# Moving a weight load, two sets of transposes and a pair of copies in a fused attention and MLP kernel

## The chip, the core and the metric

The kernel runs on one core of one Trainium2 chip. The metric is the device time of one execution in microseconds (us); lower is better. Three runs of the kernel before took 360.17, 360.77 and 361.07 us, so its median is 360.77 us.

## The reference, cut to what matters

The input x has 2048 rows of D = 576 channels in bf16. A transformer block is computed: an attention part over a short dilated window with 32 heads of 18 channels, and an MLP of 4608 hidden channels.

```python
def _A_ref(x, wqkv, wo):                       # W, dil = 8, 2
    q, k, v = split(x @ wqkv)                  # 32 heads of 18 channels
    idx = pos[:, None] - arange(W)[None, :] * dil     # 8 keys, two rows apart
    logits = einsum(q, k[idx]) * scale         # masked where idx < 0
    return einsum(softmax(logits), v[idx]) @ wo

def _B_ref(x, w1, b1, w2, b2):
    return gelu(layernorm(x) @ w1 + b1) @ w2 + b2

h = A_x + _A_ref(layernorm(A_x), A_wqkv, A_wo)
out = h + _B_ref(layernorm(h), B_w1, B_b1, B_w2, B_b2)
```

## The kernel before

**Tiles.** The 2048 rows are cut into 16 tiles j of 128 rows, where tile j holds the rows j, 16 + j, 32 + j and so on. The key that lies 2w rows back is then in tile j - 2w, on the same partition or on the one before it. The keys and values of the even tiles and of the odd tiles stand in two rings; a "halo" load, through DRAM, replaces a tile's rows by the same rows one partition down when the tiles behind it need them.

**Stages.** First come 24 "visits" on TensorE (numbered 0 to 23 in the code, each of two duos, a duo being one 128-row tile times one of Wq, Wk, Wv), until about 66 us. Into them the attention of the first two tiles, A[0] and A[1], and their LN2 are worked in. Then eight groups of two tiles pass through the MLP: MLP1 (line 228, tile `pm`) in four visits, then MLP2 (lines 605 and 693, tile `po`). Within the MLP of group k, VectorE (DVE) does the attention of group k + 1, whose tiles are named c and d in the code. Their output projection ("wo", tile `pw`) is put in the middle of group k's MLP.

**A visit.** TensorE works with its array cut into an upper and a lower half of 64 rows, which compute two banks of PSUM at once. `phase` (lines 221 to 235) issues the matmuls of one duo: phase 0 with ten matmuls, then, after phase 0 of the other duo, phase 1 with eight matmuls and the halves exchanged. Phase 1 may start only after phase 0 of the same duo has ended; that is signalled by an empty instruction in GpSimd's (POOL's) queue (`marker`, line 238). A duo ends with its eviction by ScalarE (ACT, line 322 for Q, K and V). A hook runs after all phases 0; a `between` list runs after phase 1 and the eviction of the duo that it names (a plain list: of the first duo). The duos' banks go round a ring of three, C, A, B; bank D is left to transposes and wo.

**Transposes by TensorE.** The attention output of A[0] and A[1] is transposed by `tr_o` (line 433): four blocks of 128 channels, and a last block of the channels 512 to 575, which must stand twice, once for each half of the array. For this, `o_tail` (line 197) first lets ScalarE copy these 64 channels twice into a tile `tail` of 128 columns. Ten small matmuls then fill the tile `o_pt`, and ScalarE evicts it to `oT`. The normalized h of the two tiles, `hn`, is transposed by `tr_h` (line 556), which uses `transpose_tail` (line 185): here no copy is made. Eight matmuls (line 188) transpose the four blocks, two more the channels 448 to 575, whose upper half is right, and two further ones (line 192, on a quarter of the array) overwrite the lower half with the channels 512 to 575. ScalarE evicts the tile `h_pt` to `hnT` (line 559), which the first MLP1 matmul reads for both tiles. Later tiles are stored to a DRAM scratch `td` by two DMAs (lines 210, 211: 144 KB and 16 KB) and read back by a transposing DMA (lines 216, 447, 516).

**Queues around the change.** All five engines run in the order in which the code issues instructions (`manual_schedule`). Around the change:

- Visit 16: phases 0, `tr_o(A[0])` as hook, phases 1. ScalarE has `o_tail(A[0])`, the eviction of `o_pt`, then those of the duos.
- Visits 19 and 21, `between`: LN2's root of A[0] and A[1] on GpSimd (line 161), then on ScalarE the mean (line 541) and the normalized row (line 174).
- Visit 22: phases 0, `tr_h(A[0])` as hook, phases 1; `att_exp(A[2])` on ScalarE between its two evictions. Visit 23: phases 0, `tr_h(A[1])` as hook, phases 1. MLP1 of group 0 follows.
- Group 0, second visit of MLP1: SyncE's (SP's) queue gets the store and transposed read of the attention output of c, a halo load of d, the last piece of W2 (`load_w2(6)`, 576 KB, four of the 36 row blocks of W2), then the store and transposed read of the attention output of d. A transposed read waits in the queue until the store has landed.
- Group 0, MLP2 of its first tile: before row block 0 wo of c is finished, and before row block 19 stands the visit of wo of d, which reads what the second transposed read brought. The last piece of W2 is first read at row block 32 of this tile.

Of the kernel before, what the change touches and what calls it, by code (L numbers as in the profile page):

```python
# [11 lines left out]
BF16 = mybir.dt.bfloat16  # L12
# [5 lines left out]
def kernel(  # L18
# [12 lines left out]
    nc = tc.nc  # L31
    P = 128
    _, S, D = A_x.shape
# [5 lines left out]
    KT = 5  # L39
    KF = 4  # L40
# [5 lines left out]
    HP = P // 2  # L46
# [130 lines left out]
    def transpose_in(pair, src, tail=None):  # L177
        for kt in range(KT):
            c = min(kt * P, D - P)
            block = src[:, c:c + P] if kt < KF or tail is None else tail  # L180
            for r in range(2):
                nc.tensor.matmul(pair[:, r, kt * HP:(kt + 1) * HP], lhsT=block[half_rows(r)],
                                 rhs=ident[half_rows(r), half_rows(r)], start=True, stop=True, skip_group_check=True)

    def transpose_tail(pair, src):
        for kt in range(KF):
            for r in range(2):
                nc.tensor.matmul(pair[:, r, kt * HP:(kt + 1) * HP], lhsT=src[half_rows(r), kt * P:(kt + 1) * P],
                                 rhs=ident[half_rows(r), half_rows(r)], start=True, stop=True, skip_group_check=True)
        for c, rows in ((D - P, slice(None)), (KF * P, half_rows(0))):  # L190
            for r in range(2):
                nc.tensor.matmul(pair[rows, r, KF * HP:KT * HP], lhsT=src[half_rows(r), c:c + P if rows.start is None else D],
                                 rhs=ident[half_rows(r), half_rows(r)], start=True, stop=True, skip_group_check=True)

    o_tails = {}

    def o_tail(j):
        o_tails[j] = qp.tile([P, 2, HP], BF16, tag="tail", name="tail", bufs=2)
        nc.scalar.copy(out=o_tails[j][:], in_=q_all[:, j, KF * P:D].unsqueeze(1).to_broadcast([P, 2, HP]))

    def turned(dst, pair, k0=0, k1=KT):
        return dict(out=dst[:, k0:k1, :].rearrange("p k (r t) -> p r k t", r=2),
# [15 lines left out]
    def half_rows(r):  # L218
        return slice(r * HP, (r + 1) * HP)
# [335 lines left out]

    def tr_h(j, tag):
        pair = psum_pair(tag, "h_pt")
        transpose_tail(pair, hn.pop(j)[:])
        nc.scalar.copy(**turned(hnT_slot(j), pair))

    def gelu_table():
# [143 lines left out]
    def c_(fn, *a):  # L705
        return lambda: fn(*a)
# [100 lines left out]
    with tc.manual_schedule(engines={ENG.PE, ENG.Activation, ENG.DVE, ENG.SP, ENG.Pool}):  # L807
# [93 lines left out]
        A = ATT_ORDER  # L901
# [38 lines left out]
        for v, fns in ((2, [(load_w1, 0)]), (3, [(load_w1, 1)]), (4, [(load_w1, 2)]), (6, [(load_wo, [0])]), (8, [(load_wo, [1, 2])]),  # L940
# [25 lines left out]
        between = {  # L966
            10: [c_(att_exp, A[0])],
            13: [c_(att_exp, A[1])],
            18: [c_(o_tail, A[1])],
            19: {0: [c_(ln2_rstd, A[0])], 1: [c_(ln2_norm, A[0])]},  # L970
            21: {0: [c_(ln2_rstd, A[1])], 1: [c_(ln2_norm, A[1])]},
            22: [c_(att_exp, A[2])],
        }
        wo_with = {17: A[0], 20: A[1]}
        hooks = {
            0: {1: lambda: call([c_(tr_x, EVEN[1], "C"), c_(ln1_even, 2)])},
            **{n: {m: c_(tr_x, EVEN[2 * n + m - 1], "D" if m == 1 else None) for m in (1, 2)} for n in (1, 2, 3)},
            12: c_(tr_b1, "D"),
            16: c_(tr_o, A[0], "D"),
            19: c_(tr_o, A[1], "D"),  # L980
            22: c_(tr_h, A[0], "D"),
            23: c_(tr_h, A[1], "D"),
        }
        seq = [(j, t) for t in (1, 2) for j in EVEN[:2]] + [(j, 1) for j in EVEN[2:]] \
# [53 lines left out]
        for k, g in enumerate(GROUPS):  # L1038
# [11 lines left out]
            if k == 0:  # L1050
                m1[0] += [c_(halos, 1), c_(load_w2, 5), c_(att_qk_a, d), c_(att_qk_rest, d, 1), c_(halo, d, 1)]
                mid[0] = {1: [c_(exps, d)]}
                m1[1] = [c_(pv_t, c), c_(att_den, d), c_(att_pv_a, d), c_(halo, d, 2), c_(load_w2, 6), c_(att_pv_b, d),
                         c_(dma_tr_o, d), c_(add_b2, g[0]), c_(add_b2, g[1]), c_(att_qk_a, e), c_(halo, e, 1)]
                late_wo = wo_duo(c, "B")
                ia[0] = [c_(ln2_h, c), c_(ln2_act, c), c_(put_b2, c), c_(halos, 2), c_(ln2_send, c), c_(att_qk_b, e, 0)]
                ia[19] = [lambda d=d: wo_visit((d, "A"), fill=True), c_(ln2_h, d), c_(ln2_act, d), c_(put_b2, d), c_(ln2_in, c),
                          c_(att_max, [e]), c_(att_qk_a, f), c_(ln2_send, d), c_(ln2_in, d), c_(halo, f, 1), c_(att_qk_rest, f, 1),
                          c_(exps, e, f)]
                ib[0] = [c_(finish_out, g[0]), c_(out_sum, g[0]), c_(att_den, e, f), c_(pv_sum, e), c_(send_o, e)]  # L1060
                ib[8] = [c_(read_o, e)]
            elif k == 1:
                m1[0] += [c_(att_pv_sum, d), c_(send_o, d), c_(halo, d, 2)]
                m1[1] += [c_(att_qk_a, e), c_(halo, e, 1), c_(read_o, d), c_(att_qk_b, e, 0), c_(halos, 7)]
                m1[3] += [c_(out_store, GROUPS[0][0]), c_(att_qk_a, f), c_(halo, f, 1), c_(att_qk_add, f, ((0, 0, 9), (0, 0, 4)))]
                ia[0] = [c_(wo_visit, (c, "B"), (d, "C")), c_(ln2_pair, c, d), c_(att_qk_b, f, 1, 2), c_(att_max, (e, f)),
                         c_(exps, e, f), c_(w2_sums, 0, 8, (0, 1)), c_(w2_sums, 8, 12, (0, 1)), c_(att_den, e, f)]
                ia[2] = [c_(pv_sum, e), c_(dma_tr_o, e), c_(reload_x, GROUPS[4])]
                ib[0] = [c_(finish_out, g[0]), c_(out_sum, g[0])]
# [94 lines left out]
```

## Time and profile before

| what | value |
|---|---|
| median of three runs | 360.77 us |
| the profiled execution | 361.01 us |
| its span, first to last instruction | 359.2 us |
| TensorE busy | 353.4 us (98% of the span) |
| VectorE busy | 295.8 us (82%) |
| ScalarE busy | 235.8 us (66%) |
| GpSimd busy | 47.3 us (13%) |
| granted TensorE clock | 1.000 |

The span is 1.8 us shorter than the execution that it comes from, and that execution is 0.24 us over the median. The chain of waits, the list of work followed back from the last instruction, shows VectorE from about 10 to 84 us and TensorE for nearly all that follows. In the timelines a row has its start in us, its length in us, the engine, the line, the operation with its output and inputs, how many instructions are merged into the row, and in brackets how long the engine stood idle before it and what ended that. PE is TensorE's matmuls and PEld its weight loads, SPq and POOLq are the queues in which SyncE and GpSimd issue.

### The profile page before, as it was taken

The page shows a single profiled execution, that of the slowest core. Times are in us where ns is not written, and L with a number is a line of the kernel's source. Part 1 is how long each engine was busy: PE and PEld are TensorE (multiplying, and loading weights), DVE is VectorE, ACT ScalarE, POOL GpSimd, SP SyncE. Part 2 cuts the span into 40 slices and gives each one's busy share as a digit, 9 for nine tenths or more (in the row PEclk, how much of TensorE's full clock was granted, in tenths as well). Part 3 has the DMA queues.
Part 4 walks back from the last instruction along what each step waited for, and adds up shares of the span by engine and source line. Part 5 has one row for each costly group of instructions (what it writes and reads, how often), then busy time and mean ns, then how long its engine had stood idle before and what let it go on. Part 6 is the DMA issues. An engine that isn't in the chain of part 4 may idle for free.

```text
span 359.2 us, 11579 instructions
## 1 busy us (share of the span) xinstructions
PE 353.4 (98%) x4953; PEld 289.5 (81%) x4953; DVE 295.8 (82%) x416; ACT 235.8 (66%) x524; POOL 47.3 (13%) x61
## 2 busy tenths in 40 slices
PE   8999999999999999999999999999999999999996
PEld 4777978887788877887788778877887788778874
DVE  5999999999989989998799899989998998520431
ACT  4889757897647783668566956685669566706620
POOL 2241003000212020201200211021102110210000
PEclk9999999999999999999999999999999999999999
DMA  7997799955737584722553545344555253253001
GB/s 242 328 296 168 186 248 294 387 188 137 153 71 123 164 222 84 126 71 49 118 85 82 100 110 84 77 114 108 85 90 102 57 86 56 55 120 51 4 1 34
DMA packets 63492, 46.29 MB, mean 129 GB/s; under 512 B 32192, under 2 KB 61760, under 8 KB 63440
## 3 DMA queue, kind: packets, MB, share of 16 engines
q1 hardware_dynamic: 59472, 41.50, 43.6%
q0 software_dynamic: 3744, 3.84, 9.9%
q8 instruction: 38, 0.62, 0.8%
q10 hardware_dynamic: 224, 0.22, 0.3%
q14 instruction: 14, 0.11, 0.1%
HBM read 23.38 MB, written 12.42 MB: 100 GB/s over the span
## 4 chain that ended last, share of the span: by engine, by line
PE 72%; DVE 20%; DMA 4%; SPq 1%; ACT 1%; issue 1%; DVEq 0%; ACTq 0%
PE pm L228 34%; PE po L693 25%; PE po L605 9%; PE pw L228 4%; DVE prod L361 3%; DVE ln_stats L148 3%; DVE prod L409 3%; DVE prod L352 3%; DVE prod L415 2%; DMA oT<-td 2%; DMA x_all<-in_A_x_dram 1%; ACT h_all L586 1%; SPq L104 1%; DMA td<-q_all 1%; DVE ln_mv L149 1%
## 5 line engine op out<-in xcount | busy, mean ns | idle before, releaser
L228 PE MATMUL pm<-hnT,w_sb 64*128 64x256 bf16 x2304 | 143.0, 269 | 0.0
L586 ACT ACTIVATE h_all<-pm,b_sb 128x256 f16<-128x256 f32 (+1 forms) x288 | 108.4, 495 | 51.2 <-PE pm L228 50.5
L228 PEld LDWEIGHTS <-w_sb 64*128 64x128 bf16 x2304 | 111.7, 94 | 15.1 <-issue 1.7
L693 PEld LDWEIGHTS <-h_all 128*128 128x128 f16 x480 | 46.2, 98 | 13.7 <-issue 1.6
L228 PE MATMUL pq<-wq_sb,xnT 64*128 64x288 bf16 x720 | 54.9, 283 | 0.7 <-DMA wq_sb<-in_A_wqkv_dram 0.2
L228 PEld LDWEIGHTS <-xnT 64*128 64x128 bf16 x864 | 43.4, 94 | 10.9 <-issue 1.4
L361 DVE TENSOR_TENSOR prod<-prod 128x2304 bf16<-128x2304 bf16 (+1 forms) x64 | 44.2, 691 | 2.1
L352 DVE TENSOR_TENSOR prod<-kv_ring,q_all 128x4608 bf16<-128x4608 bf16 x16 | 40.8, 2550 | 2.8 <-POOL ln_rstd L500 2.5
L409 DVE TENSOR_TENSOR prod<-kv_ring,probs 128x4608 bf16<-128x4608 bf16 x16 | 40.9, 2558 | 1.1 <-DMA kv_ring<-kv_dram 0.6
L228 PE MATMUL pm<-hnT,w1h_sb 64*128 64x256 bf16 x288 | 39.2, 269 | 0.0
L693 PE MATMUL po<-w2a_sb,h_all 128*128 128x288 bf16 (+1 forms) x262 | 35.8, 286 | 0.0
L415 DVE TENSOR_TENSOR prod<-prod 128x2304 bf16<-128x2304 bf16 (+1 forms) x32 | 33.9, 1058 | 1.1
L605 PEld LDWEIGHTS <-h_all 128*128 128x128 bf16 x288 | 27.8, 98 | 7.9 <-issue 1.0
L693 PEld LDWEIGHTS <-kv_ring 128*128 128x128 f16 x252 | 24.6, 98 | 6.3 <-DVE kv_ring L673 0.2
L605 PE MATMUL po<-w2a_sb,h_all 128*128 128x288 bf16 x224 | 28.5, 286 | 0.0
L228 PE MATMUL pq<-wqh_sb,xnT 64*128 64x288 bf16 x144 | 27.6, 283 | 0.0
L795 POOL DMA_DIRECT2D x_all<-o_sb x12 | 10.7, 888 | 126.1 <-PE pw L228 73.1
L500 POOL TENSOR_TENSOR ln_rstd<-ln_var,mhalf 128x1 f32<-128x1 f32 x13 | 10.3, 792 | 80.8 <-ACT ln_var L499 80.8
L228 PE MATMUL pw<-wo_sb,oT 64*128 64x288 bf16 x256 | 19.6, 283 | 0.7 <-DMA oT<-td 0.7
L693 PE MATMUL po<-w2b_sb,h_all 128*128 128x288 bf16 (+1 forms) x122 | 19.7, 286 | 0.1
L673 DVE TENSOR_TENSOR kv_ring<-h_all 128x1536 f16<-128x1536 f16 (+3 forms) x9 | 6.8, 760 | 15.8 <-ACT h_all L586 15.8
L161 POOL TENSOR_TENSOR ln_rstd<-ln_veps,mhalf 128x1 f32<-128x1 f32 (+2 forms) x14 | 13.2, 951 | 47.6 <-DVE ln_nmean L489 30.1
(115 smaller groups left out, 401.3 us busy)
## 6 DMA issues: line engine op xcount, KB each, us to landing
w_sb<-in_B_w_dram SPq DMA_DIRECT2D x6, 768.0 KB, 6.1
kv_ring<-kv_dram SPq DMA_DIRECT2D x28, 144.0 KB, 2.3
kv_dram<-kv_ring SPq DMA_DIRECT2D x13, 288.0 KB, 3.7
w2a_sb<-in_B_w_dram SPq DMA_DIRECT2D x3, 1008.0 KB, 10.5
x_all<-in_B_b_dram SPq DMA_DIRECT2D x15, 144.0 KB, 4.1
td<-q_all SPq DMA_DIRECT2D x14, 144.0 KB, 2.0
td<-hn SPq DMA_DIRECT2D x14, 144.0 KB, 1.8
x_all<-h POOLq DMA_DIRECT2D x14, 144.0 KB, 4.6
```

The costliest lines, as they stand in the source:

```text
L148: nc.vector.bn_stats(out=stats[:, i, c, :], in_=src[:, c * HALF:(c + 1) * HALF])
L161: nc.gpsimd.tensor_tensor(out=rstd[:], in0=veps[:], in1=mhalf[:].to_broadcast([P, n]), op=ALU.pow)
L228: last = nc.tensor.matmul(duo["g"][r ^ swap][i], lhsT=lhsT, rhs=rhs, start=(swap == 0 and i == 0 and kt == 0), stop=(swap == 1 and kt == K ...
L352: ins = nc.vector.tensor_tensor(out=prod[:], in0=k_ring[j % 2], in1=q_all[:, j, :].unsqueeze(1) .to_broadcast([P, W, D]), op=ALU.mult).ins
L361: nc.vector.tensor_tensor(out=prod[:, :, o * H:o * H + n], in0=prod[:, :, a * H:a * H + n], in1=prod[:, :, c * H:c * H + n], op=ALU.add)
L409: nc.vector.tensor_tensor(out=prod[:].rearrange("p w (d h) -> p w d h", h=H), in0=v_ring[j % 2].rearrange("p w (d h) -> p w d h", h=H), in ...
L415: nc.vector.tensor_tensor(out=prod[:, 0:n, :], in0=prod[:, 0:n, :], in1=prod[:, n:2 * n, :], op=ALU.add)
L500: ins = nc.gpsimd.tensor_tensor(out=rstd[:], in0=var[:], in1=mhalf[:], op=ALU.pow).ins
L586: pace[0] = nc.scalar.activation(out=hT(grp)[:, f, 0:N], in_=ps[:, r, i * N:(i + 1) * N], func=ACT.Gelu_apprx_tanh, bias=b1_sb[:, f:f + 1] ...
L605: nc.tensor.matmul(banks[half], lhsT=hT(grp)[:, f, i * P:(i + 1) * P], rhs=w2_rows(f)[:, half * HALF:(half + 1) * HALF], start=(f == 0), s ...
L693: nc.tensor.matmul(bank, lhsT=l, rhs=r, start=start, stop=stop, skip_group_check=True)
L795: nc.gpsimd.dma_start(out=x_of(j), in_=o_of.pop(j), accum_op=ALU.add)
```

## The change

Four things are edited:

1. `load_w2(6)` is issued after the store and the transposed read of the attention output of d, not before them.
2. `tr_o(A[0])` moves from the hook of visit 16 to its `between` list: after phase 1 and the eviction of the first duo, ahead of phase 1 of the second.
3. `tr_h(A[0])` moves in the same way within visit 22. `att_exp(A[2])` moves behind the eviction of the second duo.
4. `transpose_tail` is gone. A new `h_tail` lets GpSimd copy the last 64 channels of `hn` twice into a `tail` tile (one 128x128 bf16 copy), and `tr_h` uses the same ten matmuls as `tr_o`. The copy for A[0] stands in GpSimd's queue behind the first duo's phase 1 of visit 20, the copy for A[1] behind phase 1 of visit 22's second duo.

Most line numbers are six lower in the changed kernel; lines named in the prediction are those of the kernel before.

```diff
-    def transpose_tail(pair, src):
-        for kt in range(KF):
-            for r in range(2):
-                nc.tensor.matmul(pair[:, r, kt * HP:(kt + 1) * HP], lhsT=src[half_rows(r), kt * P:(kt + 1) * P],
-                                 rhs=ident[half_rows(r), half_rows(r)], start=True, stop=True, skip_group_check=True)
-        for c, rows in ((D - P, slice(None)), (KF * P, half_rows(0))):
-            for r in range(2):
-                nc.tensor.matmul(pair[rows, r, KF * HP:KT * HP], lhsT=src[half_rows(r), c:c + P if rows.start is None else D],
-                                 rhs=ident[half_rows(r), half_rows(r)], start=True, stop=True, skip_group_check=True)
+    def h_tail(j):
+        o_tails[j] = qp.tile([P, 2, HP], BF16, tag="tail", name="tail", bufs=2)
+        nc.gpsimd.tensor_copy(out=o_tails[j][:], in_=hn[j][:, KF * P:D].unsqueeze(1).to_broadcast([P, 2, HP]))
...
     def tr_h(j, tag):
         pair = psum_pair(tag, "h_pt")
-        transpose_tail(pair, hn.pop(j)[:])
+        transpose_in(pair, hn.pop(j)[:], o_tails.pop(j)[:].rearrange("p r c -> p (r c)"))
...
         between = {
+            16: [c_(tr_o, A[0], "D")],
             18: [c_(o_tail, A[1])],
+            20: [c_(h_tail, A[0])],
...
-            22: [c_(att_exp, A[2])],
+            22: {0: [c_(tr_h, A[0], "D")], 1: [c_(h_tail, A[1]), c_(att_exp, A[2])]},
...
         hooks = {
-            16: c_(tr_o, A[0], "D"),
-            22: c_(tr_h, A[0], "D"),
...
-                m1[1] = [c_(pv_t, c), c_(att_den, d), c_(att_pv_a, d), c_(halo, d, 2), c_(load_w2, 6), c_(att_pv_b, d),
-                         c_(dma_tr_o, d), c_(add_b2, g[0]), c_(add_b2, g[1]), c_(att_qk_a, e), c_(halo, e, 1)]
+                m1[1] = [c_(pv_t, c), c_(att_den, d), c_(att_pv_a, d), c_(halo, d, 2), c_(att_pv_b, d),
+                         c_(dma_tr_o, d), c_(load_w2, 6), c_(add_b2, g[0]), c_(add_b2, g[1]), c_(att_qk_a, e), c_(halo, e, 1)]
```

## The prediction

> **What bounds the kernel now.** I read the page's busy times first, then the chain of waits, then the timelines of the two places that the change touches.
>
> ```profile
> PE 353.4 (98%) x4953; PEld 289.5 (81%) x4953; DVE 295.8 (82%) x416; ACT 235.8 (66%) x524; POOL 47.3 (13%) x61
> ```
>
> TensorE is busy for all but 5.8 us of the span, so a gain must come from its few gaps, or from matmuls that go. The chain of waits says which gap ends last (start, length, what):
>
> ```profile
> 83.12 0.47 DVE q_all L416
> ...
> 83.99 3.19 DMA td<-q_all
> ...
> 87.24 2.77 DMA oT<-td
> ...
> 90.06 0.79 PE pw L228 x10
> ```
>
> Up to 83.6 us the end hangs on VectorE's attention, then on the way of d's attention output through DRAM, and from 90.06 on TensorE. TensorE itself waited there only a little; the queue and the weight loads show what else stood around it:
>
> ```profile
> 79.23 1.21 SPq L216 DMA_TRANSPOSE oT<-td  x1
> ...
> 81.35 0.39 SPq L104 DMA_DIRECT2D w2b_sb<-in_B_w_dram  x1
> ...
> 82.68 0.57 PEld L228 LDWEIGHTS <-oT 64*128 64x128 bf16 x10
> ...
> 84.86 4.53 PEld L605 LDWEIGHTS <-h_all 128*128 128x128 bf16 x38 [0.24 <-issue]
> ...
> 90.05 0.48 PEld L228 LDWEIGHTS <-oT 64*128 64x128 bf16 x10 [0.67 <-DMA oT<-td]
> ```
>
> At each change between the two matmul kinds the weight loads idle 0.24 us anyway ("issue"), so 0.67 - 0.24 = 0.43 us of the last row is a true wait: without it TensorE would have been at d's projection at 89.62. So two things have to come earlier, oT of d and TensorE's own arrival, and the smaller of the two shifts sets the gain.
>
> **Part 1, the W2 load behind the read.** What the load does to the store ahead of d's read (KB, us from issue to landing; first the store of c's small piece, alone, then d's, then the two W2 pieces):
>
> ```profile
> td<-q_all SPq DMA_DIRECT2D x1, 16.0 KB, 1.8
> td<-q_all SPq DMA_DIRECT2D x1, 16.0 KB, 3.2
> w2b_sb<-in_B_w_dram SPq DMA_DIRECT2D x1, 576.0 KB, 4.0
> w2b_sb<-in_B_w_dram SPq DMA_DIRECT2D x1, 576.0 KB, 8.2
> ```
>
> The W2 piece issued at 81.35 landed after 4.0 us, at 85.35, and d's store (its small piece issued at 83.99) ran into it: 3.2 us in place of 1.8. With the load behind it the store should land at 83.99 + 1.8 = 85.8, the read follows at about 85.85 in place of 87.24, and oT stands at 85.85 + 2.77 = 88.6. That is 1.0 us before TensorE's 89.62. This part alone gives the 0.43 us and no more.
>
> The price: the load goes out when the read's issue ends, 85.85 + 1.21 = 87.1, and behind it in SyncE's queue stand a halo load, the b2 load and two halo stores, which so far began behind the read, at 87.24 + 1.21 = 88.5; with 0.39 us of issue in front they now begin at about 87.5. The load is needed at row block 32:
>
> ```profile
> 93.69 2.12 PE L605 MATMUL po<-w2b_sb,h_all 128*128 128x288 bf16 x16
> ```
>
> Sixteen matmuls are row blocks 28 to 35, so block 32 starts about 0.98 us in, at 94.67, and at 93.8 if TensorE comes 0.9 us earlier. 87.1 + 4.0 = 91.1 is in time by 2.7 us; 87.1 + 8.2 = 95.3 is not. The 8.2 was measured with the queue full of W2 pieces, which is over by then, so I take 4.0 and cost it at nothing.
>
> **Part 2, the first o transposes.**
>
> ```profile
> 45.64 0.17 PEld L182 LDWEIGHTS <-q_all 64*128 64x128 bf16 x8 [0.40 <-DVE q_all L416]
> ...
> 53.61 0.28 PEld L182 LDWEIGHTS <-q_all 64*128 64x128 bf16 x8
> ...
> 53.85 2.09 PEld L228 LDWEIGHTS <-xnT 64*128 64x128 bf16 x36
> ...
> 54.23 2.86 POOL L161 TENSOR_TENSOR ln_rstd<-ln_veps,mhalf 128x1 f32<-128x1 f32 x1 [26.38 <-DVE ln_nmean L489]
> ...
> 57.46 0.87 ACT L174 ACTIVATE hn<-h,ln_nmean,ln_rstd 128x576 bf16<-128x576 f32 x1
> ...
> 58.23 0.63 ACT L322 ACTIVATE kv_ring<-pq 128x576 bf16<-128x576 f32 x1
> ...
> 58.91 2.68 PEld L228 LDWEIGHTS <-xnT 64*128 64x128 bf16 x45 [0.16 <-issue]
> ```
>
> TensorE stood 0.40 us before A[0]'s transposes, for VectorE's row, and a little more for ScalarE's tail. Half a visit on (eight matmuls of about 0.061 us, 0.49 us) both are there, as the waitless case of A[1] at 53.61 shows, where ten transposes take 0.24 us. So some 0.4 to 0.5 us go. I book nothing for it: at 58.91 TensorE waits for a bank which ScalarE frees at 58.23 + 0.63 = 58.86, behind A[0]'s normalized row, which hangs on GpSimd's root and VectorE. None of these moves, so the 0.16 us wait at 58.91 merely grows by as much.
>
> **Part 3, the LN2 transposes.** Visits 22 and 23:
>
> ```profile
> 61.61 0.29 PEld L188 LDWEIGHTS <-hn 64*128 64x128 bf16 x8
> ...
> 61.92 0.87 ACT L174 ACTIVATE hn<-h,ln_nmean,ln_rstd 128x576 bf16<-128x576 f32 x1
> ...
> 62.13 1.58 PEld L228 LDWEIGHTS <-xnT 64*128 64x128 bf16 x27
> ...
> 62.70 0.67 ACT L559 CAST hnT<-h_pt 128x640 bf16<-128x640 f32 x1
> ...
> 63.27 0.65 ACT L322 ACTIVATE q_all<-pq 128x576 bf16<-128x576 f32 x1
> ...
> 63.81 0.41 ACT L395 ACTIVATE logits<-logits 128x256 f32<-128x256 f32 x1
> ...
> 63.97 0.48 PEld L228 LDWEIGHTS <-xnT 64*128 64x128 bf16 x9 [0.27 <-issue]
> ...
> 64.12 0.65 ACT L322 ACTIVATE kv_ring<-pq 128x576 bf16<-128x576 f32 x1
> ...
> 64.46 0.29 PEld L188 LDWEIGHTS <-hn 64*128 64x128 bf16 x8
> ...
> 64.98 0.85 PEld L228 LDWEIGHTS <-xnT 64*128 64x128 bf16 x16
> ...
> 65.09 0.69 ACT L559 CAST hnT<-h_pt 128x640 bf16<-128x640 f32 x1 [0.33 <-PE h_pt L192]
> ...
> 65.86 0.44 PEld L228 LDWEIGHTS <-w_sb 64*128 64x128 bf16 x8
> ```
>
> Twelve transposes cost 62.13 - 61.61 = 0.52 us, and 0.52 again at 64.46. Ten with a tail cost the 0.24 us of above, so two times 0.28 go. And the wait of 0.27 us at 63.97, for a bank whose Q eviction ended at 63.92, goes: that eviction now comes right behind A[1]'s normalized row, at 62.70 in place of 63.27. Sum 0.28 + 0.28 + 0.27 = 0.83 us for TensorE alone, but ScalarE is next. By the spacings of these rows (cast 0.57, Q 0.54, exp 0.31, K 0.55) it does from 62.70: Q, cast, K, exp, and takes up A[1]'s cast at about 64.67, ending at 65.36. TensorE's order gives: phase 1 of the first duo 61.61 to 62.10, transposes to 62.34, phase 1 to 62.83, two phases 0 to 64.05, transposes to 64.29, two phases 1 to 65.27. MLP1 needs both: about 65.35, against 65.86. I take **0.5 us**. From there to 84.86 TensorE shows no wait, so its arrival at d's projection is 89.62 - 0.5 = 89.1; oT (88.6) is earlier.
>
> On the way lies c's projection: at 82.68 - 0.5 = 82.2 TensorE asks for oT of c, whose read, issued at 79.23, lands about 2.8 us on (d's 2.77 in the chain), at 82.0 to 82.1. This is late next: every 0.1 us that VectorE loses before 77 us is lost here.
>
> **Part 4, GpSimd's copies.** No copy is in the trace. A GpSimd instruction of that size (128x128 bf16, read and written) with nothing beside it, and a small root next to VectorE's products (the first two VectorE rows are what the copy of A[1] will meet):
>
> ```profile
> 1.08 0.29 POOL masks.py:199 TENSOR_SCALAR_AFFINE_SELECT ident<-ident 128x128 bf16<-128x128 bf16 x1
> ...
> 62.77 0.43 DVE L377 TENSOR_TENSOR logits<-logits,peak 128x256 f32<-128x256 f32 x1
> ...
> 63.11 2.55 DVE L352 TENSOR_TENSOR prod<-kv_ring,q_all 128x4608 bf16<-128x4608 bf16 x1
> ...
> 93.72 2.55 DVE L352 TENSOR_TENSOR prod<-kv_ring,q_all 128x4608 bf16<-128x4608 bf16 x1
> ...
> 95.02 1.65 POOL L500 TENSOR_TENSOR ln_rstd<-ln_var,mhalf 128x1 f32<-128x1 f32 x1 [4.11 <-ACT ln_var L499]
> ...
> 96.30 2.87 DVE L361 TENSOR_TENSOR prod<-prod 128x2304 bf16<-128x2304 bf16 x4
> ```
>
> The root that met a running product at 95.02 ended 0.40 us behind that product's end (96.67 against 96.27), although the next additions followed at 96.30, so GpSimd is let in between two VectorE instructions; the 2.86 us root of part 2 ran beside such a product too. The copy of A[0] can start at 58.4 and is used at 62.1: hidden, whatever it costs up to 3.5 us. The copy of A[1] can start at 62.79 + about 0.1; it meets the short subtraction (to 63.20), is let in ahead of the product, and ends at about 63.20 + 0.3 to 0.40 = 63.5 to 63.6. It is used at 64.2: hidden by 0.6 us. The copies also queue ahead of markers, which start phases 1, while they wait for `hn`: until 58.4 and 62.9. The next markers stand at the ends of the first phases 0 of visits 21 and 23, and are waited for only behind the second phases 0, which start at 58.91 and, by the order above, 63.4. Hidden too. What the copy costs VectorE is bounded by 0 (the adds behind the root at 96.30 took their usual 2.87) and by 0.40; I take 0.1, nearest to those rows.
>
> The Trainium skill, "SBUF — State Buffer", section "Who interferes with whom", has a rule against this part: a VectorE instruction with two SBUF inputs and a GpSimd instruction that reads SBUF exclude each other, and the second to issue fully blocks. The trace agrees where GpSimd comes second (2.86 and 1.65 us in the rows above); that VectorE blocks behind GpSimd no row shows.
>
> **The sum.** On the profiled execution's 361.01 us: 0.43 (wait for oT of d) + 0.5 (MLP1 of group 0 earlier) - 0.1 (VectorE at the copy, passed on by oT of c) = 0.83, so 360.2. After 90 us TensorE carries the chain, and VectorE, which waits for its projections, shifts with it; I let all of it through. The profiled execution lies 0.24 over the median, so I forecast 360.77 - 0.83 = **359.9 us**. Its own range is 359.6 to 360.3: no loss at the copy and 0.1 or 0.2 more from part 3, or the full 0.40 lost at the copy.
>
> **The rivals.**
>
> - **TensorE's whole 0.83 us counts.** The two phases 1 ahead of MLP1 took 65.86 - 64.98 = 0.88 us and not 16 x 0.061, so TensorE could stand at MLP1 by 65.03, and if ScalarE's five pieces close up by the same 0.3 us, the sum is 0.43 + 0.83 - 0.1 = 1.16: 359.6. Against: the spacings are already those of ScalarE without a wait.
> - **Only the wait for oT of d goes.** If A[1]'s cast on ScalarE, or oT of c, holds TensorE where it stands today, MLP1's earlier start is lost and 0.43 us remains: 360.3. For it: ScalarE has no gap from 61.92 to 65.36 by my reckoning, and oT of c is within 0.2 us. Against: Q, cast, K and exp are the same work, only reordered. The case in which the tail's ten transposes take as long as the twelve did belongs here: -0.56, of which ScalarE's limit hides most.
> - **The last W2 piece is late.** With 8.2 us it lands at 95.3, and TensorE waits 95.3 - 93.8 = 1.5 us: 359.9 + 1.5 = 361.4. For it: halo and b2 loads follow closely. Against: they are behind it in the queue. It decides from a landing of 6.7 us on.
> - **The copy of A[1] misses its gap** (slower). VectorE's product starts 0.3 us after the copy may; if the product is first, the copy waits to 63.11 + 2.55 = 65.66 and ends at 66.06. TensorE stands before the tail at 64.2 until then, starts MLP1 after 0.05 + 16 x 0.061 at 67.1, 1.2 us later than before, and loses 1.2 - 0.43 = 0.8 us at d's projection: 361.6. If GpSimd were also kept out through the four adds behind the product (2.87 us more), 364.4. Against: the root at 95.02 got in at the first boundary. It decides from a request after 63.2. This is also what that rule of the Trainium skill would do if the product were issued first.
>
> **How the numbers follow.** A difference of 0.3%, 1.08 us, is about what a measurement of this kernel can tell from no change: 359.69 and 361.85 are the bounds. Chances: forecast 0.45 (0.13 of it under 359.69); TensorE's whole 0.83 0.20 (faster); only the wait goes 0.12 (same); W2 late 0.08 (half of it beyond 361.85, when the wait passes 1.9 us); copy misses its gap 0.09 (0.04 beyond) and is kept out longer 0.06 (slower). Faster 0.13 + 0.20 = 0.33; same 0.32 + 0.12 + 0.04 + 0.05 = 0.53; slower 0.04 + 0.04 + 0.06 = 0.14. The range 359.2 to 361.7 leaves out the 364 case, the worse half of the late W2 and the largest gains, together under 0.2.
>
> **What would show it.** d's store lands within 2 us and its read is issued near 85.9; the weight load for d's projection, at 90.05 before, starts near 89.2 with 0.24 us of idle; the last W2 piece lands before 92, and no wait for it stands in TensorE's list; the first `pm` weight load is at 65.3 to 65.4; no wait of 0.4 us before the first transposes, but a longer one near 58.9; the two copies take under 0.7 us and end by 59.4 and 63.7. I am wrong if TensorE waits for GpSimd at the `tail`, if MLP1 starts no earlier, or if a wait behind 100 us grows by what was won before.

## The result and the profile after

Eight runs of the changed kernel have a median of 359.77 us (359.29 to 360.17), eight of the kernel before 360.89 us (360.17 to 361.15). The ratio is 0.9971, with a 95% interval of 0.996 to 0.9982: 0.0029 x 360.89 = 1.05 us faster, give or take 0.4. The forecast was 0.83 us, to 359.9. The difference is just inside the 0.3% that the prediction set as its bound.

The profiled execution of the changed kernel took 359.60 us. From its page, the span, the busy times and the chain of waits by engine:

```profile
span 357.8 us, 11576 instructions
...
PE 352.3 (98%) x4949; PEld 288.1 (81%) x4949; DVE 295.9 (83%) x416; ACT 235.6 (66%) x524; POOL 48.0 (13%) x63
...
PE 91%; DMA 4%; DVE 2%; SPq 1%; ACT 1%; issue 0%; ACTq 0%
```

The same chain line in the kernel before:

```profile
PE 72%; DVE 20%; DMA 4%; SPq 1%; ACT 1%; issue 1%; DVEq 0%; ACTq 0%
```

Four matmuls and 1.1 us of TensorE's time are gone, GpSimd has two instructions more, and VectorE's share of the last chain has fallen from 20% to 2%. In the kernel before, VectorE led that chain to 83.6 us. The chain in the stretch around d's projection (start, length, what) is in this profile TensorE's alone:

```profile
83.98 4.76 PE po L599 x38
88.74 0.72 PE pw L222 x10
```

Next the timeline of the changed kernel, all engines in order of time. These rows answer to those of the prediction's parts 1, 3 and 4:

```profile
42.37 3.79 PEld L222 LDWEIGHTS <-xnT 64*128 64x128 bf16 x64 [1.13 <-DMA xnT<-xd]
...
57.95 0.56 POOL L193 COPY tail<-hn 128x128 bf16<-128x128 bf16 x1 [1.29 <-ACT hn L174]
...
61.91 0.28 PEld L182 LDWEIGHTS <-hn 64*128 64x128 bf16 x8
...
62.15 1.60 PEld L222 LDWEIGHTS <-xnT 64*128 64x128 bf16 x28
...
62.47 0.49 POOL L193 COPY tail<-hn 128x128 bf16<-128x128 bf16 x1 [1.29 <-ACT hn L174]
...
62.73 2.64 DVE L346 TENSOR_TENSOR prod<-kv_ring,q_all 128x4608 bf16<-128x4608 bf16 x1
...
63.77 0.28 PEld L182 LDWEIGHTS <-hn 64*128 64x128 bf16 x8
...
64.01 0.86 PEld L222 LDWEIGHTS <-xnT 64*128 64x128 bf16 x16
...
64.26 0.70 ACT L553 CAST hnT<-h_pt 128x640 bf16<-128x640 f32 x1
...
64.90 0.44 PEld L222 LDWEIGHTS <-w_sb 64*128 64x128 bf16 x8
...
78.71 1.21 SPq L210 DMA_TRANSPOSE oT<-td  x1
...
81.73 0.58 PEld L222 LDWEIGHTS <-oT 64*128 64x128 bf16 x10
...
83.71 0.42 SPq L205 DMA_DIRECT2D td<-q_all  x1
...
85.35 1.21 SPq L210 DMA_TRANSPOSE oT<-td  x1
...
86.65 0.53 SPq L104 DMA_DIRECT2D w2b_sb<-in_B_w_dram  x1
...
88.67 0.48 PEld L222 LDWEIGHTS <-oT 64*128 64x128 bf16 x10 [0.24 <-issue]
...
90.01 0.36 PEld L222 LDWEIGHTS <-oT 64*128 64x128 bf16 x8 [0.26 <-POOLq L232]
```

A set of transposes holds up TensorE's list by 0.24 us (61.91 to 62.15, 63.77 to 64.01) where it was 0.52. MLP1 starts at 64.90, not 65.86. Between d's last store and the read stand 85.35 - 83.71 = 1.64 us, not 3.25. The weight load for d's projection has the 0.24 us of every change of matmul kind before it, and no wait for a DMA. The last row is phase 1 of d's projection. It has waited 0.26 us for a marker in GpSimd's queue, 0.02 us more than a change of kind costs. That marker stands behind the LN2 root of c, which waits for the variance of c from ScalarE (line 493), and ScalarE for VectorE's h of c (line 469). After oT of d and TensorE's own arrival this is a third thing that can hold TensorE here; below it is called the third gate.

**One zero for all traces.** The starts of two executions differ by some tenths before the changed code is reached, and by chance. So all times below are also counted from one VectorE instruction that none of the edits moves in order: the 4608-wide product that reads 63.11 in the kernel before and 62.73 here. MLP1's first weight load stood 65.86 - 63.11 = 2.75 us behind it before, and 64.90 - 62.73 = 2.17 now. d's projection stood 90.05 - 63.11 = 26.94 us behind it, and 88.67 - 62.73 = 25.94 now: 1.00 us won. The other 0.38 us of the 1.38 at that place are the earlier start. From there to the end of the span these two profiles take the same time: 359.2 - 90.05 = 269.15 us before, 357.8 - 88.67 = 269.13 now. That they agree so closely is partly luck. In the other profiles, kernel 8 left out, this stretch takes 268.56 to 270.10 us, since waits for transfers come and go in it. Near 233 us TensorE waits 0.59 us for an oT in the kernel before; in the changed kernel it waits 0.63 us there in one profile and not at all in a second one.

### The profile page after: what moved, and what is told of

It is laid out like the page before. It is cut to its first block, busy times and chain, and to the rows that moved or that the text cites. A ratio compares the mean times of both kernels' runs of the same rounds, so it can differ in the third digit from the quotient of the medians.

```text
span 357.8 us, 11576 instructions
## 1 busy us (share of the span) xinstructions
PE 352.3 (98%) x4949; PEld 288.1 (81%) x4949; DVE 295.9 (83%) x416; ACT 235.6 (66%) x524; POOL 48.0 (13%) x63
## 4 chain that ended last, share of the span: by engine, by line
PE 91%; DMA 4%; DVE 2%; SPq 1%; ACT 1%; issue 0%; ACTq 0%
PE pm L222 39%; PE po L687 25%; PE pq L222 11%; PE po L599 10%; PE pw L222 5%; DMA xnT<-xd 2%; DMA x_all<-in_A_x_dram 1%; ACT h_all L580 1%; SPq L104 1%; DVE ln_stats L148 1%; DMA oT<-td 1%; DVE q_all L846 0%; DVE kv_ring L667 0%; SPq L117 0%; DVE ln_mv L149 0%
## 5 line engine op out<-in xcount | busy, mean ns | idle before, releaser
L222 PEld LDWEIGHTS <-xnT 64*128 64x128 bf16 x864 | 41.2, 94 | 12.1 <-DMA xnT<-xd 1.1
```

Source lines behind the costliest of these rows:

```text
L222: last = nc.tensor.matmul(duo["g"][r ^ swap][i], lhsT=lhsT, rhs=rhs, start=(swap == 0 and i == 0 and kt == 0), stop=(swap == 1 and kt == K ...
```

## The experiments

The theory was the prediction's own: oT of d and TensorE's arrival at d's projection are two gates, the W2 move opens the one (0.43 us) and the LN2 transposes the other (0.5 us), the o transposes give nothing, the copies are hidden and cost VectorE a tenth. The table holds all kernels. The columns are the median, the ratio to the kernel before on the same chip with its 95% interval (the medians of the kernel before were 360.47 to 360.89 us), and the starts of MLP1 (its first weight load) and of d's projection behind the start of the product.

| kernel | median us | ratio (95%) | MLP1 | d's projection |
|---|---|---|---|---|
| before | 360.89 | 1 | 2.75 | 26.94 |
| changed | 359.77 | 0.9971 (0.996 to 0.9982) | 2.17 | 25.94 |
| changed, second time | 359.66 | 0.9969 (0.9957 to 0.9981) | 1.94, pause, 2.27 | 25.92 |
| 1: before, W2 move alone | 359.87 | 0.9976 (0.9966 to 0.9986) | 2.73 | 26.49 |
| 2: changed, W2 back | 360.60 | 1.0000 (0.9984 to 1.0016) | 1.96, pause, 2.27 | 27.04 |
| 3: changed, o transposes back | 359.26 | 0.9957 (0.994 to 0.9974) | 1.93, pause, 2.26 | 25.91 |
| 4: changed, LN2 transposes back | 360.02 | 0.9986 (0.9975 to 0.9998) | 2.72 | 26.49 |
| 5: changed, ten matmuls at the old place | 359.74 | 0.9974 (0.9963 to 0.9986) | 2.47 | 26.25 |
| 6: changed, twelve matmuls at the new place | 359.77 | 0.9982 (0.9966 to 0.9997) | 2.48 | 26.25 |
| 7: changed, tails copied by ScalarE | 359.65 | 0.9974 (0.9963 to 0.9984) | 2.48 | 26.25 |
| 8: changed, W2 later still | 361.19 | 1.0011 (0.9999 to 1.0023) | 1.95, pause, 2.27 | 25.92 |
| 9: changed, A[1]'s copy twice | 361.00 | 1.0009 (0.9999 to 1.0019) | 3.75 | 27.52 |
| 10: changed, exponentials later | 359.47 | 0.9963 (0.9951 to 0.9975) | 1.96 | 25.74 |

The intervals are 0.7 to 1.2 us wide, so the times alone do not tell a part of 0.3 us from nothing. The places in the traces do: the changed kernel's d's projection stands at 25.94 and 25.92 in two profiles, and at 25.92 in kernel 8, whose edit lies behind the product and changes nothing ahead of that projection.

### The changed kernel a second time

> The changed kernel itself, as the measure for the two others on this chip: 0.997 within 0.001; MLP1's first weight load 2.17 us and d's projection 25.94 us behind the start of VectorE's product, as in its first profile, within 0.1 us.

It was run beside kernels 8 and 10, on their chip. From its timeline:

```profile
58.86 0.72 PEld L222 LDWEIGHTS <-xnT 64*128 64x128 bf16 x13 [0.66 <-issue]
...
63.09 2.64 DVE L346 TENSOR_TENSOR prod<-kv_ring,q_all 128x4608 bf16<-128x4608 bf16 x1
...
64.60 0.70 ACT L553 CAST hnT<-h_pt 128x640 bf16<-128x640 f32 x1
...
65.03 0.09 PEld L222 LDWEIGHTS <-w_sb 64*128 64x128 bf16 x1
65.36 0.33 PEld L222 LDWEIGHTS <-w_sb 64*128 64x128 bf16 x7 [0.23 <-issue]
...
89.01 0.48 PEld L222 LDWEIGHTS <-oT 64*128 64x128 bf16 x10 [0.24 <-DMA oT<-td]
```

As expected, the ratio is 0.9969 and d's projection stands at 25.92. MLP1 is not where it was expected, at 2.17 within 0.1: it has one weight load at 1.94 us, then pauses 0.23 us and goes on at 2.27, when A[1]'s cast has ended (64.60 + 0.70 = 65.30). In the first profile TensorE came 0.2 us later to this place, so that the pause was not seen.

Behind d's projection this profile is not like the first:

```profile
90.61 0.36 PEld L222 LDWEIGHTS <-oT 64*128 64x128 bf16 x8 [0.52 <-POOLq L232]
```

VectorE waited 0.29 us for a halo load at 78.66, c's variance came 0.25 us later, counted from the product, and phase 1 of d's projection stood 0.52 us before the marker of the third gate, 0.28 more than the change of kind. It starts at 27.52 us behind the product, against 90.01 - 62.73 = 27.28 in the first profile. In the kernel before it was 91.37 - 63.11 = 28.26. So 0.98 us of the gain pass this gate in the first profile and 0.74 in this one, where the chain of waits leads through VectorE and GpSimd again.

### 1. The W2 move alone

```diff
- ... c_(halo, d, 2), c_(load_w2, 6), c_(att_pv_b, d), c_(dma_tr_o, d), ...
+ ... c_(halo, d, 2), c_(att_pv_b, d), c_(dma_tr_o, d), c_(load_w2, 6), ...
```

This is the kernel before with that line of the change.

> The kernel before with the W2 piece behind the second read alone. Two gates (the prediction's theory: TensorE's arrival at d's projection and oT of d, the later one counts): the wait of 0.43 us goes and nothing else, TensorE still starts MLP1 of group 0 as before; ratio to before 0.9988, d's projection in the trace 24.2 us behind the first pm weight load as without a wait (before: 90.05 - 65.86 = 24.19, so 23.8 now). Rival, the parts add up and W2's own cost is larger (its traffic also slowed other transfers): ratio 0.997. Rival, the load is now late at row block 32: ratio over 1.002 and a wait for it in TensorE's list.

```profile
62.80 2.55 DVE L352 TENSOR_TENSOR prod<-kv_ring,q_all 128x4608 bf16<-128x4608 bf16 x1
...
85.89 1.21 SPq L216 DMA_TRANSPOSE oT<-td  x1
...
89.29 0.48 PEld L228 LDWEIGHTS <-oT 64*128 64x128 bf16 x10 [0.24 <-issue]
```

d's projection stands at 26.49: 0.45 us better than before, by the part that TensorE had waited, and no more, although the read is issued 87.24 - 63.11 - (85.89 - 62.80) = 1.04 us earlier. The ratio, 0.9976, does not say quite the same: its interval ends at 0.9986, just short of the 0.9988 that was expected. The trace has no further gain ahead of d's projection. Behind it TensorE's wait for an oT near 233 us is 0.29 us here where it was 0.59; in the changed kernel it is 0.63 in one profile and absent in the other, so it may be chance, and whether the edit itself gains something there no run shows.

### 2. The changed kernel without the W2 move

```diff
- ... c_(halo, d, 2), c_(att_pv_b, d), c_(dma_tr_o, d), c_(load_w2, 6), ...
+ ... c_(halo, d, 2), c_(load_w2, 6), c_(att_pv_b, d), c_(dma_tr_o, d), ...
```

> The changed kernel with the W2 piece back ahead of the second store. Two gates: oT of d stands at 90.0 again, TensorE comes 0.5 to 1.0 us earlier and waits 0.9 to 1.4 us for it (weight loads idle 1.2 to 1.6 us before d's projection); all of the gain is lost, ratio 1.000 (at the lowest 0.999). Rival, the parts add up: only 0.43 us is lost, ratio 0.998.

```profile
63.05 2.64 DVE L346 TENSOR_TENSOR prod<-kv_ring,q_all 128x4608 bf16<-128x4608 bf16 x1
...
90.09 0.48 PEld L222 LDWEIGHTS <-oT 64*128 64x128 bf16 x10 [1.35 <-DMA oT<-td]
```

MLP1 is as early as in the changed kernel, and all of it is lost again: TensorE waits 1.35 us for oT in place of 0.67, and d's projection is at 27.04, 0.10 later than before. The ratio is 1.0000. The two gates are thereby shown from both sides: the W2 move alone gives 0.45 us, all the rest alone gives nothing, and together they give 1.00. The 0.10 us is close to what the product grew by (2.64 for 2.55 us); here the end hangs on VectorE, so it shows.

### 3. The o transposes back in their hook

```diff
-            16: [c_(tr_o, A[0], "D")],         # between
+            16: c_(tr_o, A[0], "D"),           # hooks
```

> The changed kernel with the first o transposes back in the hook of visit 16. The prediction's step (what is won there is lost to the bank wait at 58.9): ratio 0.997, no different from the changed kernel, the 0.4 us wait before the o transposes back and the bank wait near 58.9 at 0.16 us or less. Rival, the o transposes carry through to the end: 0.4 to 0.5 us lost, ratio 0.9985.

```profile
58.45 1.09 PEld L222 LDWEIGHTS <-xnT 64*128 64x128 bf16 x19 [0.17 <-issue]
...
62.69 2.64 DVE L346 TENSOR_TENSOR prod<-kv_ring,q_all 128x4608 bf16<-128x4608 bf16 x1
...
88.60 0.48 PEld L222 LDWEIGHTS <-oT 64*128 64x128 bf16 x10 [0.24 <-issue]
```

d's projection stands at 25.91, as in the changed kernel: the part is worth nothing. The bank wait near 58.5 shows where its gain goes. With the transposes in the hook it is 0.16 us in the kernel before and 0.17 here, with them half a visit on (the second profile of the changed kernel above) it is 0.66: what TensorE wins at 45 us, it waits 13 us later for ScalarE. One expectation failed. The wait of 0.40 us ahead of the transposes is not back; TensorE stood 0.10 us there, because in this execution it came 0.26 us later than in the kernel before, counted from the product. So part of the 0.49 us between the two bank waits is chance in this pair, and the comparison with the kernel before (0.40 us at the transposes, 0.16 at the bank) is the cleaner one. In the first profile of the changed kernel the bank wait is missing; there TensorE had lost 1.13 us at 42.37 to a DMA and so came later to the bank. The ratio of 0.9957 comes from six runs; its interval takes in the changed kernel's 0.9971, and up to d's projection the trace tells of no further gain. The profiled execution, 360.46 us, was the slowest of the six (the others took 359.01 to 359.48); behind d's projection it stood 1.14 us at 141.80 for a transposed read.

### 4. The LN2 transposes as before

```diff
+    def transpose_tail(pair, src): ...
-        transpose_in(pair, hn.pop(j)[:], o_tails.pop(j)[:].rearrange("p r c -> p (r c)"))
+        transpose_tail(pair, hn.pop(j)[:])
-            20: [c_(h_tail, A[0])],
-            22: {0: [c_(tr_h, A[0], "D")], 1: [c_(h_tail, A[1]), c_(att_exp, A[2])]},
+            22: [c_(att_exp, A[2])],           # between
+            22: c_(tr_h, A[0], "D"),           # hooks
```

> The changed kernel with the LN2 transposes of before (twelve matmuls, both in hooks, no copies by GpSimd, the exponential between the evictions). The prediction's sum: 0.5 us of earlier MLP1 lost and 0.1 us at VectorE's product won back, so 0.43 us of gain remains: ratio 0.9988, d's projection without a true wait (0.24 us idle), the first pm weight load 0.5 to 0.6 us later against VectorE's product than in the changed kernel. Rival, the o transposes bring the rest: ratio 0.9975.

```profile
62.55 2.55 DVE L356 TENSOR_TENSOR prod<-kv_ring,q_all 128x4608 bf16<-128x4608 bf16 x1
...
65.27 0.44 PEld L232 LDWEIGHTS <-w_sb 64*128 64x128 bf16 x8
...
89.04 0.48 PEld L232 LDWEIGHTS <-oT 64*128 64x128 bf16 x10 [0.24 <-issue]
```

MLP1 at 2.72 and d's projection at 26.49 are those of kernel 1, which differs from this one in the o transposes alone. The LN2 part is therefore worth 26.49 - 25.94 = 0.55 us. The next two kernels split it.

### 5. Ten matmuls at the old place

```diff
-            22: {0: [c_(tr_h, A[0], "D")], 1: [c_(h_tail, A[1]), c_(att_exp, A[2])]},
+            22: {0: [c_(att_exp, A[2])], 1: [c_(h_tail, A[1])]},
+            22: c_(tr_h, A[0], "D"),           # hooks
```

> The changed kernel with the LN2 transposes of A[0] back in the hook of visit 22 and the exponential between the evictions, but with the copied tails and ten matmuls. Times are counted from the start of VectorE's product of group 0's second tile (63.11 us before, 62.73 after), since runs differ in when the first input lands: the first pm weight load stood at +2.75 before and +2.17 after (+2.26 where TensorE was not late already), d's projection at +26.94 and +25.94. The prediction's terms: two times 0.28 us for the fewer matmuls but the first of them is lost to the wait for the bank of the Q eviction (0.27 us), which is back and a little longer, so pm at +2.45, d's projection at +26.2, ratio 0.998. Rival, the place does not matter, only the number of matmuls: pm at +2.2, ratio 0.997.

```profile
62.66 2.64 DVE L346 TENSOR_TENSOR prod<-kv_ring,q_all 128x4608 bf16<-128x4608 bf16 x1
...
63.52 0.48 PEld L222 LDWEIGHTS <-xnT 64*128 64x128 bf16 x9 [0.52 <-issue]
...
65.13 0.45 PEld L222 LDWEIGHTS <-w_sb 64*128 64x128 bf16 x8
```

The bank wait of visit 23 grows from 0.27 to 0.52 us and takes what the shorter set of A[0] gives; only the shorter set of A[1], behind that wait, counts. MLP1 at 2.47 was forecast as 2.45.

### 6. Twelve matmuls at the new place

```diff
-            20: [c_(h_tail, A[0])],
-            22: {0: [c_(tr_h, A[0], "D")], 1: [c_(h_tail, A[1]), c_(att_exp, A[2])]},
+            22: {0: [c_(tr_h, A[0], "D")], 1: [c_(att_exp, A[2])]},
```

`tr_h` uses `transpose_tail` here, as in kernel 4, and GpSimd copies nothing.

> The changed kernel with the twelve matmuls of before and no copies, but the first set half a visit on. The prediction's terms: the bank wait of 0.27 us stays away, both sets take 0.52 us each, VectorE's product is not held (2.55 us, after: 2.64): pm at +2.49 behind the product's start, d's projection at +26.3, ratio 0.998. Rival, the place does it all (ScalarE sets MLP1's start in any case): pm at +2.26, ratio 0.997.

Its product takes 2.55 us, MLP1 stands at 2.48 and d's projection at 26.25, the same as in kernel 5. So each half of the LN2 part is worth 26.49 - 26.25 = 0.24 us alone, and the other half then adds 26.25 - 25.94 = 0.31: fewer matmuls ahead of MLP1, and no wait for the bank.

### 7. The tails copied by ScalarE

```diff
-        nc.gpsimd.tensor_copy(out=o_tails[j][:], in_=hn ...)
+        nc.scalar.copy(out=o_tails[j][:], in_=hn ...)
```

> The changed kernel with the two tails copied by ScalarE in place of GpSimd, at the same places of the order. The prediction's statement that ScalarE is the next limit ahead of MLP1: the copy of A[1] stands behind the K eviction of visit 22, its transposes wait for it (0.3 to 0.6 us), A[1]'s cast comes 0.3 us later, pm at +2.5 to +2.6, VectorE's product not held (2.55 us), d's projection at +26.3; ratio 0.998. Rival, ScalarE has room: pm at +2.26, ratio 0.997, and GpSimd's copies were not needed.

```profile
62.69 2.55 DVE L346 TENSOR_TENSOR prod<-kv_ring,q_all 128x4608 bf16<-128x4608 bf16 x1
...
63.91 0.30 ACT L193 COPY tail<-hn 128x128 bf16<-128x128 bf16 x1
...
64.27 0.10 PEld L182 LDWEIGHTS <-tail 64*128 64x128 bf16 x2 [0.34 <-ACT tail L193]
```

VectorE's product is back at 2.55 us, so the 0.09 us are GpSimd's doing. But TensorE now waits 0.34 us for the tail, which stands on ScalarE behind two evictions and a cast, and d's projection is 0.31 us later than in the changed kernel. By the trace the busier engine is the worse place, although its copy is shorter (0.30 against 0.49 us); the ratios, 0.9974 and 0.9971, do not tell the two apart.

### 8. The last W2 piece later still

```diff
- ... c_(dma_tr_o, d), c_(load_w2, 6), c_(add_b2, g[0]), ...
+ ... c_(dma_tr_o, d), c_(add_b2, g[0]), ...
- ia[0] = [..., c_(halos, 2), c_(ln2_send, c), ...]
+ ia[0] = [..., c_(halos, 2), c_(load_w2, 6), c_(ln2_send, c), ...]
```

> The changed kernel with the last W2 piece issued later still: behind the two halo stores that follow d's transposed read, ahead of LN2's send of c. How much slack has it? In the changed kernel it is issued at 86.65, and row block 32, its first reader, starts near 93.3. Here it should be issued near 89.2. Theory (the piece takes 4.0 us when nothing large is before it): it lands at 93.2 to 93.8, so TensorE waits 0 to 0.5 us at row block 32, and the kernel stands at 0.997 to 0.9985. Rival (it takes 8.2 us, as in the crowded queue): it lands at 97.4, TensorE waits about 4 us there with a row that names w2b_sb, and the kernel comes out near 1.008.

From its timeline:

```profile
94.88 9.16 PEld L599 LDWEIGHTS <-h_all 128*128 128x128 bf16 x75 [1.50 <-issue]
```

The chain of waits has the transfer in it:

```profile
89.26 5.58 DMA w2b_sb<-in_B_w_dram
```

The piece took 5.58 us, more than the 4.0 of the theory and less than the rival's 8.2. TensorE's weight loads stood 1.50 us at row block 32, and 361.19 - 359.66 = 1.53 us is what the kernel lost against the changed one on the same chip: at this place nothing hides a wait. In the changed kernel the piece is issued at 86.65. With the same 5.6 us it would land at 92.25, and block 32 starts there near 93.3: an estimate of about 1 us of slack, not the 2.7 us that the prediction gave it. The trace of the changed kernel does not show the landing itself.

### 9. A second copy behind A[1]'s

```diff
-        nc.gpsimd.tensor_copy(...)
+        for _ in range(1 + (j == A[1])):
+            nc.gpsimd.tensor_copy(...)
```

The second copy writes the same values again. It forces the slower rival: a copy that is asked for while the product runs.

> The changed kernel with A[1]'s copy made twice, one behind the other, the second writing the same again. The prediction's rival of a copy that misses its gap, forced: the second copy meets VectorE's running product, ends about 0.4 us behind that product's end, the transposes wait for it, pm at about +4.0, d's projection at +27.8, 0.8 to 0.9 us behind the kernel before: ratio 1.0024. Rival, the second copy gets in with the first (GpSimd keeps the port until both are done): the product is held by some 0.2 us or more, pm at +2.3, ratio 0.997 to 0.9975.

```profile
62.33 3.07 POOL L194 COPY tail<-hn 128x128 bf16<-128x128 bf16 x2 [1.29 <-ACT hn L174]
...
62.60 2.64 DVE L347 TENSOR_TENSOR prod<-kv_ring,q_all 128x4608 bf16<-128x4608 bf16 x1
...
65.45 0.10 PEld L182 LDWEIGHTS <-tail 64*128 64x128 bf16 x2 [1.73 <-POOL tail L194]
...
90.12 0.48 PEld L223 LDWEIGHTS <-oT 64*128 64x128 bf16 x10 [0.24 <-issue]
```

The two copies took 3.07 us where one takes 0.49 (0.51 us the first, 2.50 the second, which started at 62.9), and the second ended at 65.40, just 0.16 us behind the product's end (62.60 + 2.64 = 65.24). TensorE waited 1.73 us for the tail, MLP1 is 1.00 us later than before and d's projection 27.52 - 26.94 = 0.58 later. The rival's mechanism is real, and so is its sign: ratio 1.0009 against 0.9971. Its price was set a little too high (0.8 us, by an end 0.40 us behind the product), and the 1.0024 expected here lies outside the interval (0.9999 to 1.0019). The product itself is no longer than with one copy: of two copies, one held it and one was held.

### 10. The exponentials later

```diff
-            22: {0: [c_(tr_h, A[0], "D")], 1: [c_(h_tail, A[1]), c_(att_exp, A[2])]},
+            22: {0: [c_(tr_h, A[0], "D")], 1: [c_(h_tail, A[1])]},
+            23: [c_(att_exp, A[2])],
```

> The changed kernel with the exponentials of A[2] moved on ScalarE from ahead of the cast of A[1]'s turned rows to behind the next eviction. Theory (by now TensorE's own order sets MLP1's start, since 16 matmuls of 0.061 us stand between A[1]'s transposes and it): MLP1 starts where it does in the changed kernel, 2.17 us behind the start of VectorE's product, and the ratio is 0.997 within 0.001. Rival (ScalarE's cast, which ends 0.06 us behind MLP1's first weight load, sets it): the cast is 0.31 us earlier, MLP1 starts 0.1 to 0.2 us earlier (2.0 to 2.1 behind the product's start) and the ratio is near 0.9965; this would be faster than both kernels.

```profile
62.72 2.65 DVE L346 TENSOR_TENSOR prod<-kv_ring,q_all 128x4608 bf16<-128x4608 bf16 x1
...
64.04 0.69 ACT L553 CAST hnT<-h_pt 128x640 bf16<-128x640 f32 x1
...
64.68 0.46 PEld L222 LDWEIGHTS <-w_sb 64*128 64x128 bf16 x8
...
81.56 0.54 PEld L222 LDWEIGHTS <-oT 64*128 64x128 bf16 x10
...
88.46 0.48 PEld L222 LDWEIGHTS <-oT 64*128 64x128 bf16 x10 [0.24 <-issue]
...
90.00 0.36 PEld L222 LDWEIGHTS <-oT 64*128 64x128 bf16 x8 [0.46 <-POOLq L232]
```

On MLP1's start the rival was right. The cast ends at 64.04 + 0.69 = 64.73, MLP1 goes on from its first weight load at 1.96 without the pause, and d's projection is at 25.74, 0.18 us ahead of the changed kernel beside it. So ScalarE did set MLP1's start. But the 0.18 us go no further than phase 1 of d's projection. It waits 0.46 us for the marker behind the root of c and starts at 90.00 - 62.72 = 27.28, where it also stands in the changed kernel's first profile (27.28) and in kernel 8 (27.27). The third gate has taken the gain, and so it is not shown that this kernel is the faster one: the median, 359.47 us against 359.66, does not tell them apart. The read of oT of c is close as well: it was issued at 78.72, and with a landing of 2.8 us it stood at 81.5, when TensorE asked for it at 81.56.

## Why the prediction was right

**The W2 move, 0.43 us: measured 0.45** (kernel 1). The store was alone again: 1.64 us from its issue to the read's, against 3.25. That TensorE could take only its own wait of the 1.04 us was the step that mattered, and kernel 2 shows the other side of it.

**The o transposes, nothing: measured nothing** (kernels 3 and 4). The wait moved to the bank near 58.9, from 0.16 us before to 0.66 in the changed kernel's second profile.

**The LN2 transposes, 0.5 us: measured 0.55** (kernel 4 against the changed one). TensorE's own order would have given 0.83; where ScalarE's work is moved out of the way (kernel 10), MLP1 starts 2.75 - 1.96 = 0.79 us earlier. ScalarE, named as the limit, was the limit: A[1]'s cast ended at 64.96 with MLP1 at 64.90, and taking 0.31 us of work out from ahead of it (kernel 10) brought a further 0.18 at d's projection. This also settles the rival "TensorE's whole 0.83 us counts": in this order it could not.

**VectorE at the copy, a loss of 0.1 us: the mis-sized term.** VectorE did lose 0.09 us (2.64 against 2.55), as taken, but the sum let it through by way of oT of c, and there it stayed hidden. The read of c, issued at 78.71, landed after 2.8 us, at 81.5, and TensorE asked for it at 81.73. With 0 in place of -0.1, and the two gains as measured, the sum is 0.45 + 0.55 = 1.00 us, the 1.00 us of the common zero, and 1.05 us by the ratio. The 0.09 us counts where VectorE's work is late: it is most of the 0.10 us that kernel 2 lost, and c's variance ended 89.80 - 62.73 = 27.07 us behind the start of the product, against 90.08 - 63.11 = 26.97 before. That is what the third gate waits for.

**The rest let through: right here, by a narrow margin.** The prediction took it that after 90 us VectorE shifts with TensorE. For c's LN2 it does not: as those two numbers show, it came 0.10 us later when TensorE came 1.00 us earlier. The gate at phase 1 of d's projection is in neither the sum nor the rivals. In the first profile it cost 0.02 us, in kernels 3 and 8 0.03, in the second profile 0.28, and in kernel 10 it took the 0.18.

**The number.** The forecast of 359.9 lies 0.13 us from the median, and a part of that is luck: the kernel before came out at 360.89 over eight runs and not at 360.77, which makes up for some of a gain that was larger than forecast.

The Trainium skill, "SBUF — State Buffer", section "Who interferes with whom", says that a VectorE instruction with two SBUF inputs and a GpSimd instruction that reads SBUF exclude each other and that the second to issue fully blocks. Kernel 9 agrees with it for the second copy, which came after the product had started and ended 0.16 us behind it. For the product behind the first copy, a full block would have cost the time from the product's start to the copy's end, 62.96 - 62.73 = 0.23 us in the changed kernel; measured was 0.09. The ends of GpSimd's rows are rough, so this does not refute the rule.

**The copies hidden.** They took 0.56 and 0.49 us. A[1]'s ran from 62.47, beside the short subtraction ahead of the product, and was done at 62.96, 0.8 us before its set of transposes. The rival that it misses its gap needs a request after the product's start; here it came 0.26 us before (62.47 against 62.73). That margin is small, and kernel 9 shows what lies behind it.

**The last W2 piece in time.** It was, but on a wrong price: 5.6 us of landing in that queue (kernel 8), not 4.0. The rival's own bound, a landing of 6.7 us, was 1 us away.

**The signs.** Forecast were d's read near 85.9, d's projection near 89.2 and MLP1 at 65.3 to 65.4, on the clock of the profile before. Moved by the 0.38 us of the earlier start, the changed kernel has 85.73, 89.05 and 65.28. The longer bank wait near 58.9 stands in the second profile alone.

**What stays open.** The two profiles of the changed kernel differ by the DMA wait of 1.13 us at 42 us, of which 0.23 us was left at MLP1's first weight load; what sets it was not tried. The ratio of kernel 3 is 0.0012 to 0.0014 under those of the changed kernel, and up to d's projection its trace shows nothing that answers to it; of its faster executions there is no profile. The ratio of kernel 1 stands for 0.5 to 1.2 us, more than the 0.45 us of the trace. How often the third gate costs next to nothing and how often 0.28 us is not known from so few profiles, and no run moved the marker out from behind the root.

## What to carry to other kernels

Where a step waits for two things, an edit that brings the later one forward gains only until the other stands, and an edit that brings the earlier one forward gains nothing alone (here 0.45 and 0 us, and 1.00 together): work out both arrivals, and then look for the next wait behind that step. A bulk load in a queue delays the small store behind it (here 3.25 us in place of 1.64), so it belongs behind every store and read that TensorE waits for, as far as its own deadline allows; how late that is, a run with the load moved further tells better than a duration taken from another place. Before half a visit is moved to close a gap, look for the next wait for the same engine: here one gap of 0.4 us simply reappeared 13 us later.

## What was not expected of the hardware

- A 128x128 bf16 copy on GpSimd of 0.49 us lengthened a VectorE product that started 0.26 us after it by only 0.09 us, while a copy asked for just after the product's start took until 0.16 us behind the product's end (kernel 9: 3.07 us for the two).
- Two transposes on a quarter of the array that overwrite part of a bank cost about 0.28 us of TensorE's list, more than the ten others together: 0.52 us for twelve, 0.24 for ten. Whether the quarter or the overwriting costs it was not tried.
- Pieces of W2 of 576 KB landed in 4.0, 5.6 and 8.2 us at three places of the queue.
